# Inverse feature transform in two 64-row lanes: a spectral and attention mixer on one Trainium2 core

## Chip, core and metric

The kernel runs on one core of one Trainium2 chip. The metric is the device time of one execution in microseconds (us). Before the change the median of 3 runs is 452.72 us (452.72 to 453.53).

## What is computed

The input x has 2048 rows (positions) and 640 features. Branch A is attention over 8 dilated neighbours with 32 heads, followed by a 640 x 640 projection. Branch B is a two-dimensional real Fourier transform, a product with complex weights, and the inverse transform. A gate per row mixes the two.

```python
def _B_ref(x, w_r, w_i):
    X = jnp.fft.rfft2(x, axes=(-2, -1))
    X = X * (w_r + 1j * w_i)
    return jnp.fft.irfft2(X, s=(S, D), axes=(-2, -1))

x = A_x
g = _sigmoid((x * gate_w).sum(-1, keepdims=True))
a = _A_ref(x, A_wqkv, A_wo)
b = _B_ref(x, B_w_r, B_w_i)
return g * a + (1 - g) * b
```

## The kernel before

Rows are held as 128 partitions by 16 row groups `j`. The work has four stages, which overlap.

1. `qkv` (lines 445 to 500) multiplies x by the 1920 columns of `wqkv` in three products of rounded halves each; results go to DRAM (`qkvd`). `fold` and `cols` make the first half of the forward transform beside it; its result is `zg`, a tile of 5 blocks of 128 features by 16 row groups by 128 positions.
2. `attend` computes the attention on VectorE (DVE) and GpSimd (POOL); it runs from early on until late, head by head.
3. `freq(g)` for 16 frequency groups `g`: TensorE (PE) transforms features into `u` and `v`, VectorE adds and subtracts them into `ab`, TensorE transforms across row groups into `x` and `z`, both are multiplied by the weights, and the sums and differences of the two halves, `s`, are transformed back across row groups (`g`), and ScalarE (ACT) copies them into `zg` again.
4. `spatial(j)` for 16 row groups: TensorE applies the inverse feature transform. Six matmuls `oa` and `ob` take the five 128-row blocks of `zg[:, t, j]` as stationary operands and the table `gt` as the moving one, ScalarE copies both results to `os`, and four matmuls `ha` and `hb` do the last transform along positions. `project_even` and `project_odd` apply `wo` (`woa`, `wob`), and VectorE and GpSimd add up the output.

In stage 3 `s` is one row of features per frequency: 321 sums P + z and 319 differences P - z, side by side. Five 128-column slices of `s` become the five blocks of `zg`. The sums are cosine terms, first those of the even features and then those of the odd ones, and the differences are sine terms in the same manner, so that a block's 128 rows can hold parts of two kinds. `oa` is made from the cosine terms (blocks 0 to 2) and `ob` from the sine terms (blocks 2 to 4), with all 128 rows each time; block 2 is loaded for both:

```python
mm(o1[:, 0:322], 1, gt[:, 161:483], True, False)
mm(o1[:, 0:161], 0, gt[:, 0:161], False, False)
mm(o1[:, 161:322], 2, gt[:, 483:644], False, True)
mm(o2[:, 0:322], 3, gt[:, 805:1127], True, False)
mm(o2[:, 0:161], 2, gt[:, 644:805], False, False)
mm(o2[:, 161:322], 4, gt[:, 1127:1288], False, True)
```

A float32 matmul is two matmul instructions and two weight loads on TensorE; the profile counts these ("x96" for 16 x 6 matmuls).

What each engine does in which order is not left to a scheduler. Every operation is recorded (`Plan.record`), and `order` puts them into the order that the string `ORDER` holds, a compressed list of positions; all instructions are therefore issued from one line, L385 in the profile, and are told apart by their tiles. Each engine works through its list in that order.

Of the kernel before, what the change touches and what calls it, by code (L numbers as in the profile page):

```python
# [11 lines left out]
AF = mybir.ActivationFunctionType  # L12
# [5 lines left out]
S, D = 2048, 640  # L18
# [13 lines left out]
def dft_tables():  # L32
# [6 lines left out]
    tau = 2 * np.pi  # L39
    ke, ko = PERM[:161], PERM[161:]  # L40
# [87 lines left out]
    def ck(k):  # L128
        return (np.where((k == 0) | (k == 320), 1.0, 2.0) / (S * D))[:, None]

    gt = np.zeros((640, 644))
    gt[0:161, 0:161] = np.cos(tau * np.outer(ke, d) / D) * ck(ke)
    gt[161:321, 161:322] = np.cos(tau * np.outer(ko, d) / D) * ck(ko) * (d < 160)
    gt[321:480, 322:483] = -np.sin(tau * np.outer(kb, d) / D) * ck(kb) * ((d > 0) & (d < 160))
    gt[480:640, 483:644] = -np.sin(tau * np.outer(ko, d) / D) * ck(ko) * (d > 0)
    gt = np.concatenate(
        [gt[0:128, 0:161], gt[128:256, 0:322], gt[256:384, 161:483], gt[384:512, 322:644], gt[512:640, 483:644]], 1
    )
    f = np.float32
    return {  # L140
        "t_fc": np.concatenate([fc, back[0].T, back[1].T], 1).astype(f),
# [94 lines left out]


# [18 lines left out]
class Mixer:  # L256
# [64 lines left out]
    def work(self):  # L321
# [33 lines left out]
        self.bt, self.gt = self.one("bt", 1288, tag="e0"), self.one("gt", 1288, tag="e1")  # L355
        S.dma_start(self.bt[:, 0:1122], ins["t_bt"])
# [280 lines left out]
    def freq(self, g):  # L637
# [77 lines left out]
        d0 = 321  # L715
# [7 lines left out]
        last = s[:, 640:768] if g == 0 else s[:, 512:640]  # L723
        chunks = [[(s[:, 0:128], 0)], [(s[:, 128:256], 0)], [(s[:, 256:384], 0)], [(s[:, 384:512], 1)], [(last, 1)]]
        if g == 0:
            chunks[2:4] = [[(s[:, 384:512], 1), (s[:, 256:321], 0)], [(s[:, 512:640], 1)]]
        for t0, n in ((0, 3), (3, 2)):
            o = self.ps(BG, f"g{g}_{t0}")
            for i in range(n):
                for w, back in chunks[t0 + i]:  # L730
                    m = tb[:, 1024 + 128 * back : 1152 + 128 * back] if g == 0 else tb[:, 192:320]
                    T.matmul(
                        o[0 : w.shape[1], i * 128 : i * 128 + 128],
                        w,
                        m,
                        start=(i == 0),
                        stop=(i == n - 1),
                        skip_group_check=True,
                    )
# [21 lines left out]
    def spatial(self, j):  # L761
# [2 lines left out]
        zg, gt = self.zg, self.gt  # L764
        o1, o2 = (self.ps((0, 1, 2), f"o{i}{j}") for i in "ab")

        def mm(o, t, r, start, stop):
            T.matmul(o, zg[:, t, j], r, start=start, stop=stop, skip_group_check=True)

        mm(o1[:, 0:322], 1, gt[:, 161:483], True, False)  # L770
        mm(o1[:, 0:161], 0, gt[:, 0:161], False, False)
        mm(o1[:, 161:322], 2, gt[:, 483:644], False, True)
        mm(o2[:, 0:322], 3, gt[:, 805:1127], True, False)
        mm(o2[:, 0:161], 2, gt[:, 644:805], False, False)
        mm(o2[:, 161:322], 4, gt[:, 1127:1288], False, True)
# [191 lines left out]
```

## Time and profile before

The profile is of one execution, with a span of 454.1 us from its first instruction to its last; the page gives no other time for that execution. The median of the timed runs is 1.4 us shorter.

| what | value |
|---|---|
| median of 3 runs | 452.72 us |
| span of the profiled execution | 454.1 us |
| moved by DMA, whole span | 110.75 MB, mean 244 GB/s |
| HBM read, written | 72.51 MB, 32.84 MB |
| granted TensorE clock, mean | 0.996 |
| GpSimd busy | 363.9 us (80%) |
| ScalarE busy | 211.9 us (47%) |

In the profile's lists a row names the engine, the operation and the tiles as out<-in, then shapes, the number of instructions, the busy time in us, the mean time of one in ns, and the idle time of the engine ahead of them. PE is TensorE's matmuls, PEld its weight loads, which run beside matmuls. A matmul's own duration is longer than the distance to the next one's start, since they are pipelined; what a queue of matmuls costs is read from the starts.

### The profile page before, as it was taken

To read this page: it belongs to the slowest core of one execution; us is meant where nothing else is said; L and a number is where in the kernel's file an instruction comes from. 1 tells how busy PE (TensorE), PEld (TensorE's weight loads), DVE (VectorE), ACT (ScalarE), POOL (GpSimd) and SP (SyncE) were. 2 spreads that over 40 slices of the span, in tenths; PEclk is the share of its full clock that TensorE was granted. 3 is DMA by queue.
4 is the path that set the end of the run, shared out by engine and by line. 5 is a ranking of instruction groups with operands and counts; after the bars stand their busy time and mean duration, and the time that the engine had idled before them with its cause. 6 is when DMAs were issued, how large, how long until landed. Compare 5 with 4: busy or idle time off the path is not lost. (4 is left out here: it accounts for less than half of the span.)

```text
span 454.1 us, 7249 instructions
## 1 busy us (share of the span) xinstructions
PE 441.2 (97%) x2440; PEld 391.8 (86%) x2440; DVE 409.8 (90%) x519; ACT 211.9 (47%) x561; POOL 363.9 (80%) x316
## 2 busy tenths in 40 slices
PE   9999999999999999999998989999989999999996
PEld 6888888888889888899886769998877899999996
DVE  4899999899999999999978989999999997899484
ACT  4723165625226463255356666667554655342110
POOL 1158895899899898988977898976899998889810
PEclk9999999999999999999998999999999999999999
DMA  8998999887968979679979778989883331365932
GB/s 312 401 383 268 340 330 377 305 264 237 272 183 272 340 217 316 181 216 320 303 220 294 240 230 250 297 245 320 258 257 105 85 97 54 118 207 134 296 123 87
DMA packets 73956, 110.75 MB, mean 244 GB/s; under 512 B 21296, under 2 KB 50992, under 8 KB 73920
## 3 DMA queue, kind: packets, MB, share of 16 engines
q1 hardware_dynamic: 40192, 69.32, 46.8%
q10 hardware_dynamic: 32816, 36.97, 26.1%
q0 software_dynamic: 912, 4.00, 2.4%
q8 instruction: 19, 0.31, 0.3%
q14 instruction: 17, 0.14, 0.1%
HBM read 72.51 MB, written 32.84 MB: 232 GB/s over the span
## 5 line engine op out<-in xcount | busy, mean ns | idle before, releaser
L385 PE MATMUL qkv<-w,xo 128*128 128x480 f32 (+1 forms) x480 | 110.6, 385 | 0.0
L385 PE MATMUL qkv<-w,xe 128*128 128x480 f32 (+1 forms) x474 | 104.3, 382 | 0.0
L385 PEld LDWEIGHTS qkv<-w,xe 128*128 128x128 f32 x474 | 89.3, 189 | 15.2 <-ACT xe L385 0.9
L385 PEld LDWEIGHTS qkv<-w,xo 128*128 128x128 f32 x480 | 89.7, 189 | 13.8 <-ACT zg L385 0.2
L385 ACT COPY ev<-qkv 128x480 f32<-128x480 f32 x64 | 34.9, 558 | 48.3 <-PE qkv L385 35.9
L385 PE MATMUL woa<-wo,oT 128*128 128x320 f32 x240 | 47.2, 318 | 0.4 <-ACT oT L385 0.4
L385 PE MATMUL wob<-wo,oT 128*128 128x320 f32 x240 | 46.9, 315 | 0.2 <-ACT ya L385 0.2
L385 POOL TENSOR_TENSOR P<-P,wp 128x963 f32<-128x963 f32 (+1 forms) x16 | 35.4, 2212 | 6.6 <-DMA P<-X 4.0
L385 PEld LDWEIGHTS woa<-wo,oT 128*128 128x128 f32 x240 | 37.7, 188 | 1.1 <-ACT oT L385 0.6
L385 PEld LDWEIGHTS wob<-wo,oT 128*128 128x128 f32 x240 | 37.8, 188 | 0.6 <-ACT ya L385 0.4
L385 POOL TENSOR_TENSOR fx<-fx 128x160 f32<-128x160 f32 (+1 forms) x16 | 12.8, 818 | 24.2 <-DMA fc<-in_t_fc 17.1
L385 POOL TENSOR_TENSOR w<-raw,w 128x480 fp32r<-128x480 f32 (+1 forms) x20 | 24.8, 1262 | 5.3 <-ACT w L385 5.3
L385 ACT CAST oT<-oTp 128x384 fp32r<-128x384 f32 (+1 forms) x32 | 13.4, 427 | 30.9 <-PE oTp L385 17.3
L385 PEld LDWEIGHTS g<-mm,s 128*128 128x128 f32 x150 | 21.0, 190 | 7.1 <-ACT zg L385 5.0
L385 PE MATMUL g<-mm,s 128*128 128x128 f32 x150 | 23.5, 280 | 3.1 <-ACT zg L385 3.0
L385 DVE TENSOR_TENSOR oT<-oTp,oT 128x384 fp32r<-128x384 f32 (+1 forms) x32 | 15.2, 485 | 11.0 <-ACT oT L385 10.7
L385 PE MATMUL oa<-gt,zg 128*128 128x161 f32 (+1 forms) x96 | 24.0, 344 | 0.0
L385 PE MATMUL ob<-gt,zg 128*128 128x161 f32 (+1 forms) x96 | 22.0, 344 | 0.0
L385 PE MATMUL u<-bt,zc 128*128 128x240 f32 (+2 forms) x96 | 21.1, 335 | 0.7 <-DVE ab L385 0.7
L385 PE MATMUL v<-bt,zc 128*128 128x240 f32 (+2 forms) x96 | 21.5, 335 | 0.2
L385 DVE TENSOR_TENSOR fx<-fx 128x642 f32<-128x642 f32 (+2 forms) x24 | 19.2, 798 | 0.7
L385 PEld LDWEIGHTS u<-bt,zc 128*128 128x128 f32 x96 | 16.9, 199 | 2.9 <-PE g L385 0.9
(304 smaller groups left out, 1107.6 us busy)
## 6 DMA issues: line engine op xcount, KB each, us to landing
qkvd<-ev ACTq DMA_DIRECT2D x32, 480.0 KB, 4.8
wp<-in_ws SPq DMA_DIRECT2D x16, 642.0 KB, 5.9
raw<-in_wqkv SPq DMA_DIRECT2D x25, 240.0 KB, 5.9
fx<-in_x SPq DMA_DIRECT2D x8, 641.0 KB, 7.9
ot<-od SPq DMA_DIRECT2D x16, 320.0 KB, 3.9
P<-X ACTq DMA_DIRECT2D x30, 160.5 KB, 4.6
fd<-fx POOLq DMA_DIRECT2D x6, 640.0 KB, 5.6
f<-fd SPq DMA_DIRECT2D x6, 640.0 KB, 6.1
```

Of the source, the lines that this page charges most:

```text
L385: p.dve.memset(w, 0.0)
```

## The change

The inverse feature transform of stage 4 is laid out anew. Even features and odd features form two lanes of 64 rows: each of the five blocks of `zg` now holds 64 even-feature rows in partitions 0 to 63 and 64 odd-feature rows in partitions 64 to 127. `oa` is made from the lower 64 rows of all five blocks, `ob` from the upper 64 rows. That makes ten matmuls of 64 rows where there were six of 128 rows. Before, the six matmuls of a row group have 1288 output columns in all; now each lane's five have 966, both lanes' ten 1932. `oa` and `ob` still lie in PSUM banks of their own. `gt` is shortened from 1288 to 966 columns, the two copies into `os` keep their number.

To give `zg` that layout, stage 3 writes `s` in four pieces rather than two: 256 sums, 32 + 32 differences, 32 + 32 sums, 256 differences; the zeroth sum is written by one ScalarE activation of a single column. Group 0 clears two 128-column pieces and writes its differences one parity at a time. The number of `g` matmuls stays.

The order string is another one.

```diff
+STRIPS = (2, 0, 322), (0, 0, 161), (1, 0, 161), (3, 161, 161), (4, 161, 161)
...
 ORDER = """
-T>t<81poj4|NsC0{{R31`zHT%QmDPk&^9H>y=H*?`Lk%9Gnl%)B_CdQV7rLsIrdLM6sJFoVB8Rk|2U=URH5DLwHy3}>N|I2375U5sNENOZ_r>p;QjNS0Qt^d&3_BFn1BL!{U(U9<aW#`
...
+{Wp48S^xk5{}S0j0stWa8~^|S5YJf5;2m=f99;ka0sAKZbW*6j%FQ!El~cU`6eXsx^(m8QmuIkq#|cH@ab~Jn4egv)CIlEHgj+~6SGMaZ?}mn0k-S+`iIg>hnOfzJ?024dK1+{_s&$Fa?USIGCMp69
...
+        plus, mixed, minus = (s[:, 128 * t : 128 * t + 128 * n] for t, n in ((0, 2), (2, 1), (3, 2)))
+        plus, minus = (q.rearrange("p (t b r) -> p b t r", t=2, b=2) for q in (plus, minus))
+        mixed = mixed.rearrange("p (b r) -> p b r", b=2)
+        V.tensor_add(plus, strips(P[:, 0], 0), strips(z, 0))
         if g == 0:
-            d0 = 449
-            G.memset(s[:, 384:449], 0.0)
-        V.tensor_add(s[:, 0:321], P[:, 0], z)
-        V.tensor_sub(s[:, d0 : d0 + 319], P[:, 0, 2:], z[:, 2:])
+            other = s[:, 640:768].rearrange("p (b r) -> p b r", b=2)
+            G.memset(s[:, 256:384], 0.0)
+            G.memset(s[:, 640:768], 0.0)
+            for b in range(2):
+                V.tensor_sub(other[:, b, 33 - b : 64], parity(P[:, 0], 1 - b, 31 + b)[:, b], parity(z, 1 - b, 31 + b)[:, b])
+        else:
+            V.tensor_sub(mixed[:, :, 32:64], parity(P[:, 0], 0, 32), parity(z, 0, 32))
+        V.tensor_add(mixed[:, :, 0:32], parity(P[:, 0], 128, 32), parity(z, 128, 32))
+        V.tensor_sub(minus, strips(P[:, 0], 32), strips(z, 32))
+        A.activation(out=s[:, 288:289], in_=z[:, 0:1], func=AF.Identity, bias=P[:, 0, 0:1])
...
-        mm(o1[:, 0:322], 1, gt[:, 161:483], True, False)
...
+        c = 0
+        for t, a, n in STRIPS:
+            for o, k in ((o1, slice(0, 64)), (o2, slice(64, 128))):
+                T.matmul(
+                    o[:, a : a + n], zg[k, t, j], gt[k, c : c + n], start=(t == 2), stop=(t == 4), skip_group_check=True
+                )
+            c += n
         os = self.osr.next(f"os{j}", 644)
-        oq = os.rearrange("p (b a d) -> p a b d", b=2, a=2)
-        A.copy(oq[:, 0], o1[:, 0:322].rearrange("p (b d) -> p b d", b=2))
-        A.copy(oq[:, 1], o2[:, 0:322].rearrange("p (b d) -> p b d", b=2))
+        A.copy(os[:, 0:322], o1[:, 0:322])
+        A.copy(os[:, 322:644], o2[:, 0:322])
```

The order on TensorE at the start of stage 4, before the change. `oa1` is the result `oa` of row group j = 1, `g15` belongs to the last frequency group, the number behind an underscore is the buffer's; the last word is the size of the output:

```order
L385 MATMUL g15_3_815<-mm13_771,s15_813 128x128 x2
L385 MATMUL oa1_872<-gt_327,zg_211 128x322
L385 MATMUL oa1_872<-gt_327,zg_211 128x161 x2
L385 MATMUL oa3_878<-gt_327,zg_211 128x322
L385 MATMUL ob1_873<-gt_327,zg_211 128x322
L385 MATMUL ob1_873<-gt_327,zg_211 128x161 x2
L385 MATMUL oa3_878<-gt_327,zg_211 128x161 x2
L385 MATMUL ha1_875<-os1_874,fct_71 128x161
L385 MATMUL ob3_879<-gt_327,zg_211 128x322
```

The same place on TensorE in the changed kernel, where every `oa` and `ob` row is a matmul of 64 rows:

```order
L385 MATMUL oa3_878<-gt_327,zg_211 128x322
L385 MATMUL oa3_878<-gt_327,zg_211 128x161
L385 MATMUL g15_3_815<-mm13_771,s15_813 128x128
L385 MATMUL oa1_872<-gt_327,zg_211 128x322
L385 MATMUL g15_3_815<-mm13_771,s15_813 128x128
L385 MATMUL oTp0_860<-ident_69,ot12_858 128x128
L385 MATMUL ob1_873<-gt_327,zg_211 128x322
L385 MATMUL oa1_872<-gt_327,zg_211 128x161 x4
L385 MATMUL ob1_873<-gt_327,zg_211 128x161 x3
L385 MATMUL oa3_878<-gt_327,zg_211 128x161
L385 MATMUL ob1_873<-gt_327,zg_211 128x161
L385 MATMUL oa3_878<-gt_327,zg_211 128x161
```

The code emits the lanes in turn, `oa`, `ob`, `oa`, `ob`; the order string does not keep that. Here `oa1` has four of its matmuls in a row, and 128-row matmuls (`g15`, `oTp0`) stand between 64-row ones. Over the whole program the ten matmuls of the 16 row groups make 160; behind 40 of them the next TensorE matmul is one of the other lane, behind 78 one of the same lane, and behind 42 a matmul of 128 rows. TensorE changes 84 times between 64-row and 128-row matmuls.

On VectorE, the place in stage 3 where group 8's `s` is made, before the change (`L5a`, `o6a0` and `pv6a0` are attention, `oT4` is a projection's transpose):

```order
L385 TENSOR_TENSOR z9_729<-z9_729,wp9_718 128x321
L385 TENSOR_REDUCE o6a0_510<-pv6a0_511 128x160
L385 TENSOR_TENSOR z8_716<-z8_716,P8_714 128x321
L385 TENSOR_TENSOR s8_726<-P8_714,z8_716 128x321
L385 TENSOR_TENSOR s8_726<-P8_714,z8_716 128x319
L385 TENSOR_REDUCE L5a_535<-pr5a4_538 128x2x8x4
```

And in the changed kernel:

```order
L385 TENSOR_REDUCE o6a0_510<-pv6a0_511 128x160
L385 TENSOR_TENSOR z8_716<-z8_716,P8_714 128x321
L385 TENSOR_TENSOR s8_726<-P8_714,z8_716 128x2x2x64
L385 TENSOR_TENSOR s8_726<-P8_714,z8_716 128x2x32
L385 TENSOR_TENSOR s8_726<-P8_714,z8_716 128x2x2x64
L385 TENSOR_TENSOR s8_726<-P8_714,z8_716 128x2x32
L385 TENSOR_REDUCE L5a_535<-pr5a4_538 128x2x8x4
```

What stands around the group's `s` is the same; two instructions have become four.

More of the change, by code (lines that the diff above doesn't have):

```diff
@@ L129, in ck @@
         return (np.where((k == 0) | (k == 320), 1.0, 2.0) / (S * D))[:, None]
[L131 to L138, printed above, removed]
+    lanes = np.zeros((2, 320, 322))
+    for lane, k, fits in ((0, PERM[1:161], (d > 0) & (d < 160)), (1, ko, d > 0)):
+        c = np.cos(tau * np.outer(k, d) / D) * ck(k) * ((d < 160) | (lane == 0))
+        s = -np.sin(tau * np.outer(k, d) / D) * ck(k) * fits
+        lanes[lane, 0:160, 0:161], lanes[lane, 160:320, 161:322] = c, s
+    lanes[0, 160] = np.repeat([1.0, 0.0], 161) / (S * D)
+    lanes = lanes.reshape(2, 5, 64, 322)
+    gt = np.concatenate([lanes[:, t, :, a : a + n].reshape(128, n) for t, a, n in STRIPS], 1)
     f = np.float32
@@ new lines @@
+PX7ALwn0<wZc-XUI@uX1mU#xt`{)!LYce^&ssP;n?EzePgxk9JYd-{y%QQy;6@U0P+@zPBuvj7-t=45W#JdGDHIopEeO-jU%d(DaB*?`~N2mvs|1sUot0s7}VMrBB#eDFDo1RKH`%ZVCAxAl3(^&}7
+=ii?a-c4VPi7pf#6?m=5bcslwsyM3(R8$%(MJtAn_Uay(Im|tR^~RuuetfDSu^OE{tfa6ps`>u^-kX`B#A~Vwsc%SjY;Jv92jN3lgge|M0vo2qX)bXSpjst7E>PIJ<7MEo%zVLW&X?8{G4=k07HU|a
+*MB}kJYv|NIbH5jPR0w-0Fa4K>I-_70~`#r(KRi^7WJrck|i_3^8gN95G9AXi4lNxH=tv50Oxq7r{pPjmK#$_p#v6^rnt-ge<m+NSkr_@vcHb6MXsjb?W55?t9?PjGDmpF#nG~xLUBY<#IB>k!h$C!
+z-hlt+~emyEO0bO{wwJEu1hR3X1@N0OrQxh{JF$lk}G3NGs%?Yg#!@iY8_EH7!(?|4h|x;tC|ye+sgvGErvgz0esf}QvSK!V<W(<VfxlLS&4~}O`Bk0{oQyhED2T(^C#jqPq!2(`dv=hHRXC?DG029
@@ new lines @@
+SLk6^a_aagp?qPWw@h5GUtaNZ&W&Bj8fsg6^0)ykAEdVUHu~dkqQz~s?J*y0XyY7m&e2o<4i_=Q0#iEbAi7WG1FM|jik?-qV)4y!?9rePIO#p`BXZX*@r*QUL%z6H+$jP!{aVZm_rW+PbfI{9bG*U?
+E_LINx}Qna>NY+WBy4?@jhjD=la(qlzBu?W$|nb!jA$dZ-?H4`6$Q&w`N~!ZeO+mgilZS?4hij#%}oqVUXoE<Pblzkdc<6|_77YecmZD2Tg-0!H6snUTdLYCZVrNVu<X^Sh}J$|!9HGI_gki@@!oYb
+c4wLL50)gM?0juDa}iV3@FJm+NVn9Vs$3m61ycd31-y?kN{<RAdAOHWx$*HvG^p93wpc%naJrrMa>fV(DF7o}7%YSpO(sbtu4-fo6hNAOTd);|!L$CzhR+=Hf*jY`F!e30j#$*$;Q)Z&C-h~7m=O<R
+fjSLesvd}MFN%#rz%9yh%V6CFi2)X|8&!a^uXS^-5+Dz;BgC--$QFdndlcJ}x=myp!sjM~9tN1)Gb77g>UT5D05%2%-@g+RnEpaadJ#4Py3Qv}L5%N_SXpUuTJH!`0SM@u*h9t$eE-|R%mNLEm;(qs
@@ new lines @@
+uyj39*(7WO{+@C){tWJiHK+1eH4IEvha9nJm}{<iH2>4_UT2#!Li8j@1xqDi#Wp&s@C+VfdqMMlg>cIPOdof~zzvANxeA1%O;s{)#g~{NP_$Yna;Q`LYzlE5orJ=$uC}dhb*ffVv`Ng6e~bDe!(vya
+A9{8KX7mR#!a}~8<#?fxEye_3fTTM43mhddtO8&6isL=MD34oI_-)P*AfC4AVzS0Q?mUeVONAl&F-ijQMPx}tAU<*%mcz<M)Kud>S^ik151vBL%=7%StnMzBYjr@@ihnvR_~Ke{5{hi;J1*PRa9f8P
+cf{tPut3EXfiAw#VBY9x0MAWLa{oADt{4ZSey4!=iu$b`<HXdv0I?SgFg||D2dR9v=v(H9E3aMVyFxtX9zJ#M#q8}?N+{P%l8QWVW|3A1k67584Nvh#kdCjVc5O!+;-!nPPdDE6T(3-Y@bSM+VgHt^
+xZw_S6@%Rf$pL>I%p9Q;>B;_FjwPrab<uIXx_ZB7Fuyv=khT6^+d#6T@|G>_WIkC<Q)h`AxwMC^+`pBX@@pwRL-Ts5tpXt3b9B4Z3<ruB(HupyzD)MIcBcw74!XpjjGlW{VAdSd4To|Ac%rJ)Z67|u
@@ new lines @@
+`b_Bs5RS{WkWL4-t<u_OO0L(I-&zr~G-3Q0&CF&u(1F`YWedb=>~XE1Eh=KEd+k=_)R2B0;P_aen3$+Y%#*M%Z-b~Dq<;HUY%&2}HJFKNc@)MP!t6s^y$tMG733C~T<!y#!<E5mgNuPAS7~?cK@}B_
+$xTpaxh^#|add$WS1z5dt|f}*DNka~bbvi&V<y~i9nuioNR4K4zM+!)0G1fpD;%n#s3*irf6tDad7qU!D%VZTD^?!G0T}~CYCt%mU4zq^6MM&LHRBHu-`zgW51yn>=!97yh)7BjhKc+yuFt<KUL=^j
+s90G+PUsk~tp^iqelS4lhT!>mC<^{2Bz?@SAvF-AIwCzfF0_k+;DyYam@35NBWWhchi`r|u9@M-L9)wUC);%}fj%U6&smz{4&Z158Pr#OY(){xh(YeOijOD|?o7vpG5Qk%q7aP*3X67E+9U?dTo3_%
+OhBtc#S&NE-odH$dXI2h=GbsO57Ns1onb0!_*ld|2(0nCbzuSbbYi#>&txzrqZa7Eup?8MkprbK8WX1A?pC$^3aDYk^B44^2sv32i_S7+e6Nn}Sw*?LK&SY%jCoP(^zrc(gz@tg6tMA=E~sK4H}ebm
@@ new lines @@
+Yx6`jtOV1lwULSH-rcwzn^%t76@dUQov5+W`X{0iz}qQO8I3W&1d!r!>5rEr!q4AxRh1^qdA`5Ki~H5O$6^(fH3O6UM4@jO^XdO?3YAOKvN+-D0enc7!AWr?I7Gr4i4?I=$oC$Q@=z@&j(~F8J<IG3
+2aRj3Hfur$9dJhL8JzionfUczGlv8WpsKs}MOCmIGid2&*R9|en!i_XXR8U@n-n$G;SD5tVT~CNbSVL(KL^Ls2{Y^pJD%H|8zHHh9wSl&y6>Lm&>>>6Xnwr#e=NP&Q?&#r$24f@e17F%$N10+W`|la
+O%_$H@Qtzk%=kB;&%XwRV`kJSAH|1x_Ku5N**gJ&OB!Q0#b*-9kv-uS5nd;>8f$}SG<&AMx=1tj)nZCC$BlN8^6JDFJqxxktod*I4A5Vp`H8Z((Nt43>%eaPY#0Qwg43eS<om(Ds~_c~#>$o}6YFgP
++w8vX%L^GJoYqvY)TUMxy*i>7EQ>y<Ge7Ns6h|@yY6r(~-B8=}q?NG$kv!t%mEK2}zC|o5Oiwe8POu|nMo9m3U#G}J$iG3ZuL2b_gTOcd<MPRKQ(V#IE%2x{?)!kppDvm$ZOS3J9}UeKZXPHVZ#ki`
@@ new lines @@
+-Ma{L0BwyV*v_V9Vp6JYA+xp;O?+&@agHN}#!tYU0r`LmIa|L8l;j5l7Pc%k@Y>zbmk#dK1y?peo9?rel;N{45vkL{+J30!Xq!ipgaR^+wFaJps#zBqzlxyso~+8E?{-cZsDIEnG)SSUtZp=u8%fO0
+x#z-KrE`@E;TO^L8&UUC(x}AwM<f`qT|0^F)#C&1HW5kwIkY23kpt=c&0b>f*RhW+47rj@;F==oSaG+y9IZYZ7B|d@Je&A_+;j+<MeR#(TEO8WIUxD8lXhbF#fHKqKDfe;xQozxH+V#}7l;?1Lrq9t
+;-xb|+AFP$Oa;-ou2&8LBffSVvzV*M_FR1byB-z9@%u%t)-aBY^}>mqqsJOT+1+MZv&A&8q?$A}w%_{>Pa8Kz?d$fbG?X9+vm{rzjz-^#q8pak^KtdHr{z5=(pljljw}`cTeX4|tq<9mE%?!8SkiSF
+z<c{e441L_pl`j+h~yJ;lla;tU=e<$G{S;Gq9Zh|GYENB(}hK9EVc2-F4S)^Si?E?Bj>-PydaGMk}(d<S3r&*8p|6L^5;p*Xc)e!*zIPA<_kYy<$)MA{;6mt_WyZmgF~S&gvo=n`=Na#>o`-=W>09!
@@ L235 @@
+KPXOqH<$%PPC*HYQL2_1V1h=yrM2>Sia5KKBhf+XJYyN@o%-VfsYSLDJ!>)Ed--@im0`D%ELn1NE37TJZA37uJXQe`gH{PUZ}J(FyeQEiL@c1stf(5QN7HSeO;@iczt+qkJ%in(?jNCu?)RUbRyoqv
+`D16Tk8)c4|Ij8O5SOZp855l%7Huf?Z9`qNRWkur9U_2?J+<W*Y&_r{GA)TZyi`(#%H_Z<;`nQ=|Hd@&{ct2lE-8SS^%Z~xswN|PGhQ)Vg^knG4z}PX^z~lfT(@;bO$q0+>8sg-st{g_zKvWr=W-@u
+7ibO4^CC=zgKx~}_2ys$yiEjVG)97Z%+w_S00FQX^f~|lJ*hX-r~nH50ssI2003E9
 """
@@ L354, in work @@
         S.dma_start(self.sign, ins["t_sign"])
-        self.bt, self.gt = self.one("bt", 1288, tag="e0"), self.one("gt", 1288, tag="e1")
-        S.dma_start(self.bt[:, 0:1122], ins["t_bt"])
+        self.bt, self.gt = self.one("bt", 1122, tag="e0"), self.one("gt", 966, tag="e1")
+        S.dma_start(self.bt, ins["t_bt"])
         S.dma_start(self.gt, ins["t_gt"])
@@ L714, in freq, with parity, strips @@
         s = self.s12r.next(f"s{g}", 768)
-        d0 = 321
-        if g == 0:
-            d0 = 449
-            G.memset(s[:, 384:449], 0.0)
-        V.tensor_add(s[:, 0:321], P[:, 0], z)
-        V.tensor_sub(s[:, d0 : d0 + 319], P[:, 0, 2:], z[:, 2:])
+        def parity(a, k, n):
+            return a[:, 1:321].rearrange("p (b k) -> p b k", b=2)[:, :, k : k + n]
+        def strips(a, k):
+            return parity(a, k, 128).rearrange("p b (t r) -> p b t r", t=2)
+        plus, mixed, minus = (s[:, 128 * t : 128 * t + 128 * n] for t, n in ((0, 2), (2, 1), (3, 2)))
+        plus, minus = (q.rearrange("p (t b r) -> p b t r", t=2, b=2) for q in (plus, minus))
+        mixed = mixed.rearrange("p (b r) -> p b r", b=2)
+        V.tensor_add(plus, strips(P[:, 0], 0), strips(z, 0))
+        if g == 0:
+            other = s[:, 640:768].rearrange("p (b r) -> p b r", b=2)
[8 more added lines that the diff above has]
+        A.activation(out=s[:, 288:289], in_=z[:, 0:1], func=AF.Identity, bias=P[:, 0, 0:1])
         yield
[L723 to L726, printed above, removed]
         for t0, n in ((0, 3), (3, 2)):
@@ L729, in freq @@
             for i in range(n):
-                for w, back in chunks[t0 + i]:
+                for t, back in (((0, 0),), ((1, 0),), ((2, 0), (5, 1)), ((3, 1),), ((4, 1),))[t0 + i][: 2 if g == 0 else 1]:
                     m = tb[:, 1024 + 128 * back : 1152 + 128 * back] if g == 0 else tb[:, 192:320]
                     T.matmul(
-                        o[0 : w.shape[1], i * 128 : i * 128 + 128],
-                        w,
+                        o[:, i * 128 : i * 128 + 128],
+                        s[:, 128 * t : 128 * t + 128],
                         m,
```

39 lines of the change are left out of this document (2 added, 37 removed).

## Prediction

> **What bounds the kernel now.** I read the head of the page first, then the chain of work that ended last, then the busy time of each engine by stage.
>
> ```profile
> span 454.1 us, 7249 instructions
> PE 441.2 (97%) x2440; PEld 391.8 (86%) x2440; DVE 409.8 (90%) x519; ACT 211.9 (47%) x561; POOL 363.9 (80%) x316
> ...
> by line: PE woa L385 6.9%; PE wob L385 6.4%; PE oa L385 3.8%; PE ob L385 3.8%; PE hb L385 1.9%; PE ha L385 1.9%; PE g L385 1.8%; PE oTp L385 1.2%; DMA P<-X 0.7%; PE v L385 0.7%; DVE o6a L385 0.6%; ACTq L385 0.6%; DVE pr5b L385 0.6%; PE x L3
> ...
> core 0: us, PE busy (x) PEld busy (x) DVE busy (x) ACT busy (x) POOL busy (x), PEclk, DMA share, GB/s
> 0.00:220.00 220.00, 218.94 (x1068) 189.91 (x1069) 206.22 (x207) 99.07 (x250) 177.91 (x163) 1.00 0.87 291
> 220.00:347.40 127.40, 119.83 (x706) 105.57 (x705) 117.51 (x173) 76.22 (x217) 109.32 (x85) 0.99 0.84 259
> 347.40:409.00 61.60, 61.60 (x386) 56.26 (x385) 55.28 (x75) 29.88 (x78) 54.71 (x45) 1.00 0.34 103
> 409.00:454.10 45.10, 40.84 (x286) 40.02 (x284) 30.78 (x68) 6.68 (x16) 22.00 (x25) 1.00 0.51 161
> ```
>
> TensorE (PE) is busy for 441.2 of 454.1 us, and the chain's shares are nearly all PE rows. The last four rows split the span where the change splits it: the qkv stage (to 220), the frequency groups (220 to 347.4), the inverse feature transform with its last step (347.4 to 409), and the last projections. From 347.4 to 409 PE is busy 61.60 of 61.60 us: **each us that its `oa` and `ob` matmuls gain or lose there is a us of the kernel**, until another engine takes over. The next is VectorE (DVE) with 55.28 us. From 220 to 347.4 neither is full: PE has 7.6 us idle, DVE 9.9 us.
>
> **The matmuls of the inverse transform.** What one costs is the distance between starts:
>
> ```profile
> start us, us, engine line op out<-in xcount [idle before <-releaser]
> 378.07 0.44 PE L385 MATMUL hb<-os,fct 128*128 128x161 f32 x2
> 378.34 0.43 PE L385 MATMUL oa<-gt,zg 128*128 128x161 f32 x2
> 378.61 0.44 PE L385 MATMUL ha<-os,fct 128*128 128x161 f32 x2
> 378.89 0.70 PE L385 MATMUL oa<-gt,zg 128*128 128x322 f32 x2
> 379.43 0.71 PE L385 MATMUL hb<-os,fct 128*128 128x161 f32 x4
> ```
>
> A pair of instructions (one float32 matmul) of 161 columns takes 378.34 to 378.61, 0.27 us; one of 322 columns takes 378.89 to 379.43, 0.54 us. Before, `oa` has one wide and two narrow matmuls in each of 16 row groups, and `ob` the same: 32 x (0.54 + 2 x 0.27) = 34.6 us, and the chain's 3.8% + 3.8% of 454.1 us is 34.5 us. The change removes these and adds, for each lane and row group, one wide and four narrow ones of 64 rows: 32 x (0.54 + 4 x 0.27) = 51.8 us if they run one behind the other, 25.9 us if the two lanes always run side by side. So this part lies **between +17.2 and -8.7 us**. No row of the trace shows a matmul of 64 rows, so both ends stand; the order decides where between them it falls.
>
> Between, I take a walk through the changed order with two rules: a matmul instruction starts no earlier than the one ahead of it on PE, and no earlier than its own lane is free; one of 128 rows needs both. The first rule is what the rows above show, where each instruction starts as the last one's 0.135 us are over, in the program's order. Then four `oa1` in a row hide nothing: `ob1` behind them starts when the last instruction of the fourth starts. Only at a change of lane does an instruction of the one run beside the last of the other. There are 40 such changes; each hides one instruction, 0.135 us where both are narrow and up to 0.27 where both are wide; walked through, 6.2 us in all. 51.8 - 6.2 = 45.6 us, or **+11.0 us** against 34.6. Lanes in strict turn would have hidden almost half of 51.8; the order, with 78 same-lane successors against 40, does not let them. I take the walk, since it uses the spacing of the nearest rows and their order.
>
> A rule speaks about the two assumptions. The Trainium skill ("TensorE: Matmul & The Clock Gate", section "The mechanism") says that matmuls of different row groups overlap, starting some 4 ns apart, and that matmuls start and end in program order. No run here shows the first; by both together the sum is the walk's.
>
> Weight loads grow from 12 to 20 instructions per row group, and could become a bound themselves:
>
> ```profile
> L385 PEld LDWEIGHTS oa<-gt,zg x96: 187/190/192, 347.4 to 406.9; 128*128 128x128 f32 x96
> L385 PE MATMUL oa<-gt,zg 128*128 128x161 f32 x64 | 13.5, 299 | 0.0
> L385 ACT COPY z<-qkv 128x1 f32<-128x1 f32 x16 | 2.5, 162 | 1.7 <-ACT ev L385 1.7
> ```
>
> A load takes 190 ns and there is one every 135 ns already, with no idle PE time in the `oa` row (0.0), so loads are pipelined as well. Beside the run of one lane they are hidden as now; where two lanes do pair, two loads are needed in 135 ns, which no row shows. At worst the pairing then hides nothing: that is the +17.2 end.
>
> **The group sums.** Distances between starts on DVE:
>
> ```profile
> 337.04 0.42 DVE L385 TENSOR_TENSOR oT<-oTp,oT 128x256 fp32r<-128x256 f32 x1 [0.38 <-ACT oT L385]
> 337.38 0.49 DVE L385 TENSOR_TENSOR z<-z,wp 128x321 f32<-128x321 f32 x1
> ...
> 339.97 0.87 DVE L385 TENSOR_TENSOR s<-P,z 128x321 f32<-128x321 f32 x2
> 340.76 0.41 DVE L385 TENSOR_REDUCE s5a<-L5a 128x32 f32<-128x256 f32 x1
> ...
> 342.48 0.34 DVE L385 RECIPROCAL s5a<-s5a 128x32 f32<-128x32 f32 x1
> 342.74 1.43 DVE L385 TENSOR_TENSOR pr4a<-kt4a,qbank 128x1280 f32<-128x1280 f32 x1
> ```
>
> Two instructions of 321 and 319 columns take 339.97 to 340.76, 0.79 us. In their place come two of 256 (0.34 each, 337.04 to 337.38) and two of 64. For 64 I extrapolate: 0.395 for 320 and 0.34 for 256 columns make 0.055 per 64 columns, so 0.34 - 3 x 0.055 = 0.18; the shortest small one in these rows, 32 columns, takes 0.26, which I take as the upper end. A group costs 2 x 0.34 + 2 x 0.18 = 1.04 us, +0.25 (up to +0.41); 16 groups +4.0 us (0 to 6.6). DVE has 9.9 us idle in that stage and waits for other engines in some of it, while PE waits for DVE in other places; the front shows that nothing else moved around `s`. I put **+1.4 us** of the 4.0 on the path, a third, with 0 and 6.6 as ends. What stands behind `s` on DVE is attention (`L5a`), which GpSimd and the odd projections wait for; that work has room in the longer stage that follows.
>
> The 16 one-column activations on ScalarE are 16 x 0.162 = 2.6 us by the row of the one-column copy `z<-qkv`. ScalarE is busy 76.22 of 127.40 us there; behind each stand copies into `zg` and `zc`, so 0 to 2.6, and I take 0 (inside the 1.4). The copies into `os` keep number and size; the 128-column memsets on GpSimd run once, and GpSimd has 18 us idle in that stage: 0. `gt` is a quarter shorter and loaded long ahead: 0. The qkv stage has the same instructions in another order, PE busy 218.94 of 220: 0, ends -1 and +1.
>
> **Sum.** +11.0 + 1.4 = +12.4 us in the profiled execution, 454.1 to 466.5; the median of the runs stands 1.4 us below the span, so **465.1 us**.
>
> **Rivals.**
> 1. *The lanes do not overlap at all* (two loads in 135 ns do not fit, or float32 pairs block each other; then the change doesn't do what its name says). Against it only that nothing in the trace forbids it. +17.2 + 1.4: **471.3**.
> 2. *Switching between 64-row and 128-row matmuls empties the array.* TensorE changes 84 times. An `oa` instruction lasts 299 ns in the row above and the next starts after 135; if the next had to wait for the end, that is 0.164 us each, 84 x 0.164 = 13.8 us on top of the walk: **478.9**. The trace has no such switch. The Trainium skill ("TensorEngine Tiling (Array Packing)", section "Key Properties") says that a change of tiling mode drains TensorE; by that rule this rival is the forecast, without it the walk is, and no run here shows it yet.
> 3. *Lanes with queues of their own*, each running ahead of the other between two matmuls of 128 rows. Walked through so, 13.3 us are hidden rather than 6.2, and `oa` and `ob` cost 38.5 us, +3.9: **458.0**. Against it: PE's rows start in program order.
> 4. *Faster: each 64-row matmul costs half, whatever the order*, because PE takes matmuls of the idle lane from far behind in its queue, past 128-row ones. -8.7 on PE; but DVE, with 55.28 of 61.60 us, then ends the stage: at most -6.3, and +1.4: **447.8**. It decides from the point at which more than 17.2 + 1.4 = 18.6 of the 25.9 us that can be hidden are hidden. For it: weight loads run ahead of matmuls already (PEld busy 56.26 us beside a full PE), so PE looks ahead in some way; against it: rival 3's reason, and the 84 barriers.
>
> **How the numbers follow.** The walk gets 0.42, no overlap 0.17, draining 0.14, own queues 0.10, half cost 0.14, and 0.03 is left for a new order that gains or loses elsewhere (PE has 12.9 us idle in the span, which a better order could use). The forecast is the likeliest case, 465.1. The range 455 to 480 holds the first four (0.83) with the bounds of the sums below and above them, but for the case that draining and the upper bounds meet; it leaves out the faster case. A measurement of this kernel can tell about 0.2% from no change (0.9 us; the three runs lie 0.8 apart). Slower: 0.82; within 0.2%: 0.03 (something between rivals 3 and 4); faster: 0.15.
>
> **What would show it.** If the walk is right, `oa` and `ob` starts in the new trace lie 0.135 us apart within a run of one lane, two starts come nearly together only at a change of lane, and the stage from the first `oa` to the last `ha` grows by about 11 us with PE full. No pairs of near starts at all: rival 1. A gap of some 0.16 us whenever a `woa`, `ha` or `g` follows an `oa` or `ob`: rival 2. Starts of 64-row instructions 0.07 us apart on average: rival 4, and the forecast is wrong on its main term. `s` rows: four per group with about 1.04 us from first start to the next instruction. If PE idles more than 2 us longer between 220 us and the first `oa`, the 1.4 was too small.

## Result and profile after

The changed kernel takes 479.92 us (median of 4 runs, 479.33 to 481.69) against 453.12 us: the ratio is 1.0593, 95% interval 1.057 to 1.0616. It is 26.8 us slower. The forecast was 465.1 us, 12.4 us slower; the direction was right, the size less than half.

The head of the changed kernel's page:

```profile
span 477.6 us, 7544 instructions
PE 464.9 (97%) x2568; PEld 398.0 (83%) x2568; DVE 411.7 (86%) x552; ACT 215.3 (45%) x577; POOL 362.1 (76%) x317
```

Its busy time by stage; the columns are those of the windows shown before, with the borders moved to the first `oa` and the last `ha`:

```profile
core 0: us, PE busy (x) PEld busy (x) DVE busy (x) ACT busy (x) POOL busy (x), PEclk, DMA share, GB/s
0.00:220.00 220.00, 216.37 (x1051) 186.58 (x1052) 203.58 (x203) 95.34 (x237) 172.63 (x161) 1.00 0.88 286
220.00:348.60 128.60, 123.29 (x720) 105.80 (x718) 123.59 (x209) 82.41 (x244) 114.35 (x90) 1.00 0.87 263
348.60:434.60 86.00, 86.00 (x527) 66.84 (x527) 54.52 (x76) 31.84 (x82) 53.50 (x43) 1.00 0.25 78
434.60:477.60 43.00, 39.26 (x274) 38.80 (x273) 30.05 (x66) 5.68 (x15) 21.64 (x25) 1.00 0.55 169
```

The loss is in one row. The inverse transform took 62.5 us before (first `oa` at 347.5, end of the last `ha` at 410.0) and takes 86.0 us now, with TensorE full in both; the stages ahead of it are 1.1 us longer, the one behind it 1.1 us shorter. That makes 23.5 us of span. The timed runs differ by 26.8. The changed kernel's profiled run took 479.33 us for a span of 477.6, 1.7 us more; by the same step (an estimate) the span of before belongs to a run of 455.8 us, 2.7 above the median. The granted TensorE clock of before, the third number from the end, has a dip ahead of the inverse transform that the changed kernel's profile does not have:

```profile
240.00:260.00 20.00, 17.81 (x86) 14.99 (x87) 18.17 (x29) 12.65 (x38) 15.33 (x15) 0.91 0.89 276
```

If those 2.7 us were lost ahead of the transform, the stages there have really grown by 3.8 us rather than 1.1; the profiles do not settle it. Of the runs below, two of the four of e4_same took 528.9 and 529.8 us at a mean granted clock of 0.93 and 0.92, of which there is no profile, and its time, stage and ratio are those of the other two.

What happened to the matmuls shows in the timeline of TensorE. Rows are start, length, engine, operation and tiles; `ha` and `hb` have 128 rows, `oa` and `ob` 64:

```profile
361.18 0.82 PE L385 MATMUL hb<-os,fct 128*128 128x161 f32 x4
361.93 0.54 PE L385 MATMUL ob<-gt,zg 64*128 64x322 f32 x1
361.94 0.54 PE L385 MATMUL oa<-gt,zg 64*128 64x161 f32 x2
362.31 0.43 PE L385 MATMUL ob<-gt,zg 64*128 64x322 f32 x1
362.31 0.43 PE L385 MATMUL oa<-gt,zg 64*128 64x161 f32 x2
362.58 0.98 PE L385 MATMUL ob<-gt,zg 64*128 64x161 f32 x6
...
366.18 0.54 PE L385 MATMUL ha<-os,fct 128*128 128x161 f32 x2
366.65 0.54 PE L385 MATMUL oa<-gt,zg 64*128 64x161 f32 x2
367.12 0.82 PE L385 MATMUL hb<-os,fct 128*128 128x161 f32 x4
```

Two things stand here. At 361.93 and 361.94 both lanes start 7 ns apart: they do run side by side, and `ob`'s second instruction (362.31) starts after `oa`'s second, though it stands ahead of it in the program. And around a change between 128 and 64 rows things are slow: `ha` at 366.18 and `oa` at 366.65 are single narrow matmuls, which took 0.27 us from start to start before; each takes 0.47 us here. The weight loads of the same place, with their idle time in brackets:

```profile
366.18 0.30 PEld L385 LDWEIGHTS ha<-os,fct 128*128 128x128 f32 x2 [0.17 <-issue]
366.65 0.29 PEld L385 LDWEIGHTS oa<-gt,zg 64*128 64x128 f32 x2 [0.17 <-issue]
367.12 0.57 PEld L385 LDWEIGHTS hb<-os,fct 128*128 128x128 f32 x4 [0.17 <-issue]
```

The load of each first matmul behind a change starts with that matmul and not ahead of it, after 0.17 us without any load. The load no longer hides behind the matmul before. In the rows of the tile `oa` (shortest, median and longest in ns; x96 are 16 x 3 float32 matmuls of two instructions) this is the maximum. The kernel before:

```profile
L385 PE MATMUL oa<-gt,zg x96: 297/300/437, 347.5 to 407.0; 128*128 128x161 f32 x64, 128*128 128x322 f32 x32
```

The changed kernel:

```profile
L385 PE MATMUL oa<-gt,zg x160: 294/298/536, 348.6 to 431.9; 64*128 64x161 f32 x128, 64*128 64x322 f32 x32
```

A wide instruction lasts 535 or 536 ns behind a change, where the longest of before lasted 437: 0.10 us of a weight load waited for. The other 0.09 us lie ahead of it, in which nothing starts: `ha` at 366.18 and `oa` at 366.65 are 0.47 us apart: 0.27, 0.10 for the load and 0.09, rounded. Together a change costs about 0.19 us, and there are 84.

### The profile page after: what moved, and what is told of

Same layout as the page of the kernel before. It is cut to its first block, busy times and chain, and to the rows that moved or that the text cites. A ratio compares the mean times of both kernels' runs of the same rounds, so it can differ in the third digit from the quotient of the medians.

```text
span 477.6 us, 7544 instructions
## 1 busy us (share of the span) xinstructions
PE 464.9 (97%) x2568; PEld 398.0 (83%) x2568; DVE 411.7 (86%) x552; ACT 215.3 (45%) x577; POOL 362.1 (76%) x317
## 4 chain that ended last, share of the span: by engine, by line
PE 76%; DVE 5%; POOL 4%; DMA 2%; ACT 2%; issue 2%; ACTq 0%; POOLq 0%; SPq 0%; DVEq 0%
PE qkv L385 33%; PE woa L385 7%; PE wob L385 7%; PE oa L385 5%; PE ob L385 5%; PE z L385 5%; DVE fx L385 3%; PE g L385 3%; PE hb L385 2%; POOL P L385 2%; PE ha L385 2%; PE u L385 2%; PE oTp L385 2%; PE v L385 2%; DMA wp<-in_ws 2%
## 5 line engine op out<-in xcount | busy, mean ns | idle before, releaser
L385 PE MATMUL qkv<-w,xo 128*128 128x480 f32 (+1 forms) x480 | 116.0, 389 | 0.0
L385 PE MATMUL qkv<-w,xe 128*128 128x480 f32 (+1 forms) x474 | 106.3, 383 | 2.6 <-ACT ev L385 1.8
L385 PEld LDWEIGHTS qkv<-w,xo 128*128 128x128 f32 x480 | 88.5, 189 | 12.8 <-ACT zg L385 0.2
L385 PE MATMUL wob<-wo,oT 128*128 128x320 f32 x240 | 49.6, 324 | 0.6 <-ACT ya L385 0.6
L385 PE MATMUL oa<-gt,zg 64*128 64x161 f32 (+1 forms) x160 | 34.7, 344 | 0.6 <-ACT zg L385 0.6
L385 PE MATMUL ob<-gt,zg 64*128 64x161 f32 (+1 forms) x160 | 34.5, 345 | 0.0
L385 POOL TENSOR_TENSOR fx<-fx 128x160 f32<-128x160 f32 (+1 forms) x16 | 11.7, 741 | 22.4 <-DVE fx L385 19.4
L385 PEld LDWEIGHTS oa<-gt,zg 64*128 64x128 f32 x160 | 23.5, 186 | 5.7 <-issue 3.1
L385 ACT CAST oT<-oTp 128x384 fp32r<-128x384 f32 (+1 forms) x32 | 13.3, 428 | 32.9 <-PE oTp L385 32.0
L385 PEld LDWEIGHTS ob<-gt,zg 64*128 64x128 f32 x160 | 23.6, 186 | 4.6 <-issue 3.2
L385 PE MATMUL g<-mm,s 128*128 128x128 f32 x150 | 25.4, 282 | 0.8 <-ACT zg L385 0.8
```

What stands on the lines that cost most here:

```text
L385: p.dve.memset(w, 0.0)
```

## Experiments

All times of a run are medians (of e4_same both); ratios are to runs of the kernel before on the same chip beside them, which took 453.1 to 454.2 us. The stage is from the first `oa` to the end of the last `ha` or `hb` in the run's profile, as above.

| run | time, us | ratio, 95% interval | stage, us | changes 64/128 rows |
|---|---|---|---|---|
| before | 453.12 | 1 | 62.5 | none |
| changed | 479.92 | 1.0593 (1.057 to 1.0616) | 86.0 | 84 |
| e1_turns | 465.99 | 1.0249 (1.0179 to 1.032) | 70.8 | 30 |
| e2_runs | 492.75 | 1.0839 (1.0771 to 1.0907) | 98.0 | 30 |
| e3_full | 475.82 | 1.0471 (1.041 to 1.0532) | 81.1 | none |
| e4_same | 490.1, 491.0 | 1.0792 (1.0696 to 1.0888) | 97.2 | 84 |
| e5_pipe | 461.85 | 1.0166 (1.0124 to 1.0208) | 67.9 | 30 |
| e6_split4 | 455.67 | 1.0034 (1.0007 to 1.0062) | 62.5 | none |
| e7_old_order | 466.71 | 1.0261 (1.0216 to 1.0306) | 69.0 | 30 |
| e8_copies | 463.28 | 1.0192 (1.0157 to 1.0226) | 67.0 | 30 |
| e9_old_copies | 460.24 | 1.0151 (1.0122 to 1.0181) | 63.9 | 30 |

### e1_turns: the lanes in turn, nothing between

TensorE's order, the first row group (the other engines' order stays):

```diff
-L385 MATMUL ob1_873<-gt_327,zg_211 128x322
-L385 MATMUL oa1_872<-gt_327,zg_211 128x161 x4
-L385 MATMUL ob1_873<-gt_327,zg_211 128x161 x3
+L385 MATMUL oa1_872<-gt_327,zg_211 128x322
+L385 MATMUL ob1_873<-gt_327,zg_211 128x322
+L385 MATMUL oa1_872<-gt_327,zg_211 128x161
+L385 MATMUL ob1_873<-gt_327,zg_211 128x161
...
```

> The changed kernel with one thing different: the ten 64-row matmuls of each row group stand together on TensorE, the two lanes in turn, with no 128-row matmul among them (30 changes between 64-row and 128-row matmuls in place of 84; nothing else is moved). Theory A (lanes run from queues of their own between 128-row matmuls, and every change costs about 0.195 us: 0.09 us in which the array empties and 0.105 us of an exposed weight load): oa and ob cost 26.0 + 30 x 0.195 = 31.9 us against 38.7 + 84 x 0.195 = 55.1 in the changed kernel, so 479.9 - 23.2 = about 457. Theory B (program order holds between lanes, a change of lane hides one instruction, changes cost what then remains, 0.11 us): 28.2 + 3.3 = 31.5, about the same; the next run tells them apart. Theory C (the loss lies elsewhere, in the new order of the other engines): at most 5 us faster than the changed kernel.

465.99 us: 13.9 us faster than the changed kernel, but 9 us short of theory A; theory C is out. The timeline of its first row group:

```profile
350.53 0.27 PE L389 MATMUL oTp<-ident,ot 128*128 128x128 f32 x1
350.74 0.54 PE L389 MATMUL oa<-gt,zg 64*128 64x322 f32 x1
350.74 0.54 PE L389 MATMUL ob<-gt,zg 64*128 64x322 f32 x1
351.11 0.43 PE L389 MATMUL oa<-gt,zg 64*128 64x322 f32 x1
351.12 0.43 PE L389 MATMUL ob<-gt,zg 64*128 64x322 f32 x1
351.38 0.30 PE L389 MATMUL oa<-gt,zg 64*128 64x161 f32 x1
351.39 0.30 PE L389 MATMUL ob<-gt,zg 64*128 64x161 f32 x1
...
352.35 0.29 PE L389 MATMUL ob<-gt,zg 64*128 64x161 f32 x1
353.16 0.54 PE L389 MATMUL ha<-os,fct 128*128 128x161 f32 x2 [0.51 <-ACT os L389]
```

In turn, the lanes lose nothing: 20 instructions start in pairs, and the group, from its first start until the last pair at 352.35 has had its 0.135 us, takes 1.75 us, 1.63 us of it the sum of one lane (one wide and four narrow matmuls) and 0.10 us the first weight load. The first step, 350.74 to 351.11, is 0.37 us where a wide instruction takes 0.27. What theory A had not counted is the last row: `ha` waits for ScalarE's copy into `os`, 0.51 us, since nothing stands between any more. TensorE is idle for 6.4 us in this stage, where before it has no such wait: 2.6 us end with a copy into `os`, 2.8 us with ScalarE's scalings `ho` and `h` of the last results, 1.0 us with other work. Starts of `ha` and `hb` lie 219 and 201 ns from the next start on average, changes included; before it is 136.

### e2_runs: one lane first, then the other

```diff
-for t, a, n in STRIPS:
-    for o, k in ((o1, slice(0, 64)), (o2, slice(64, 128))):
+for o, k in ((o1, slice(0, 64)), (o2, slice(64, 128))):
+    for t, a, n in STRIPS:
```

(The order string does it; these lines say what it amounts to.)

> As the run before (30 changes, matmuls of a row group together), but the five of one lane first and then the five of the other. Theory A (queues of their own): the second lane's matmuls start beside the first lane's, as fast as in turns: about 457. Theory B (program order holds, only one instruction in each group is hidden): oa and ob cost 16 x (3.26 - 0.14) + 30 x 0.11 = 53 us, about 478.

492.75 us. Queues of unlimited depth are out. The first row group:

```profile
351.55 1.50 PE L391 MATMUL oa<-gt,zg 64*128 64x322 f32 x7
352.75 0.54 PE L391 MATMUL ob<-gt,zg 64*128 64x322 f32 x1
352.88 0.43 PE L391 MATMUL oa<-gt,zg 64*128 64x161 f32 x2
353.13 0.43 PE L391 MATMUL ob<-gt,zg 64*128 64x322 f32 x1
353.16 0.29 PE L391 MATMUL oa<-gt,zg 64*128 64x161 f32 x1
353.40 1.26 PE L391 MATMUL ob<-gt,zg 64*128 64x161 f32 x8
```

Seven of ten `oa` instructions start alone; `ob` comes in when three are left. All 14 groups of this run that stand alone start in this pattern: **here TensorE looks ahead past three waiting matmul instructions of the busy lane, no more**. (Whether their weight loads count too, no run tells.) A group takes 2.95 us in place of 1.75. Per group the run lies between the theories (1.75 and 3.12 us), near theory B; its time is 15 us beyond theory B's 478, since the waits of e1_turns and a lower clock come on top.

At full clock the order of the lanes explains 18 us of the 26.8 between this run and e1_turns. Most of the rest is the clock: three groups of the stretch below take 4.7, 5.6 and 5.6 us rather than 2.95, 7 us in all.

```profile
370.00:380.00 10.00, 8.77 (x47) 7.42 (x46) 7.59 (x7) 1.99 (x7) 7.37 (x6) 0.83 0.00 0
380.00:390.00 10.00, 10.00 (x34) 8.02 (x34) 0.00 (x0) 3.15 (x8) 1.84 (x2) 0.50 0.20 49
390.00:400.00 10.00, 10.00 (x37) 9.05 (x37) 8.79 (x7) 0.71 (x4) 4.65 (x4) 0.50 0.07 18
```

The third number from the end is the granted clock of TensorE: 0.50 for 20 us, with TensorE shown busy throughout. In the changed kernel's profile it is 1.00 in every stage.

### e3_full and e4_same: overlap and changes apart

```diff
 # e3_full
-o[:, a : a + n], zg[k, t, j], gt[k, c : c + n], start=(t == 2), stop=(t == 4), skip_group_check=True
+o[:, a : a + n], zg[:, t, j], gt[:, c : c + n], start=(t == 2), stop=(t == 4), skip_group_check=True
 # e4_same
-for o, k in ((o1, slice(0, 64)), (o2, slice(64, 128))):
+for o, k in ((o1, slice(0, 64)), (o2, slice(0, 64))):
```

> The changed kernel and order, but the ten matmuls of a row group take all 128 rows of zg and gt, so that both lanes' products are added up in both results (the inverse transform's values are left out in that sense); the number, width and place of the matmuls stay. No lane can run beside another and there is no change between 64 and 128 rows. Theory A: oa and ob cost 32 x 1.628 = 52.1 us against 55.1, 3 us faster than the changed kernel: about 477. If changes cost nothing (my prediction's walk), 52.1 against 45.6: 6 us slower, about 486. If a change costs 0.16 us on top of the walk: 52.1 against 59.4, 7 us faster, about 472.5.

> The changed kernel and order, but both results are made from the lower 64 rows of zg and gt, so that the odd features are left out and the even ones are computed twice; number, width and place of the matmuls stay, and the 84 changes stay, but there is one lane only and nothing can run side by side. Theory A: 52.1 + 84 x 0.195 = 68.5 us against 55.1, 13.4 us slower than the changed kernel: about 493. The distance to the run with all 128 rows is the price of 84 changes: 16.4 us by theory A, 0 if changes are free, 9 by theory B.

e3_full takes 475.82 us, 4.1 less than the changed kernel; e4_same takes about 490.5. Both are near theory A. The rows of the tiles `oa` and `ha` of e3_full:

```profile
L385 PE MATMUL oa<-gt,zg x160: 297/300/538, 350.0 to 428.7; 128*128 128x161 f32 x128, 128*128 128x322 f32 x32
L385 PE MATMUL ha<-os,fct x64: 297/300/303, 355.4 to 430.9; 128*128 128x161 f32 x64
```

And of e4_same:

```profile
L385 PE MATMUL oa<-gt,zg x160: 294/297/536, 349.1 to 443.6; 64*128 64x161 f32 x128, 64*128 64x322 f32 x32
L385 PE MATMUL ha<-os,fct x64: 297/300/404, 355.2 to 445.9; 128*128 128x161 f32 x64
```

`ha` is the same matmul in both. Its maximum is 303 ns among 128-row matmuls and 404 ns behind 64-row ones: the change costs in both directions. (The 538 ns of e3_full are the first `oa`, which had waited 0.57 us for `zg`, so that its load too started with it.) With the same instructions in the same places, the stages are 81.1 us without changes and 97.2 us with 84 of them: 16.1 us, **0.19 us per change**; 0.09 and 0.10 us, read from the starts and lengths, make the same. The changed kernel has 86.0 with the 84 changes and two lanes: the overlap hides 97.2 - 86.0 = **11.2 us**. And with all 128 rows, one behind the other, the stage is 81.1 - 62.5 = **18.6 us** longer than with the six matmuls of before. 17.0 us of this are the matmuls themselves: from start to next start `oa` and `ob` take 34.5 us before and 51.5 in e3_full. The rest is other work, since the new order has nine more matmul instructions `oTp` and `g` inside this stage (about 1.0 us). 18.6 + 16.1 - 11.2 = 23.5 us, the whole difference of the stage.

### e6_split4: the four sums alone

```diff
-        V.tensor_add(s[:, 0:321], P[:, 0], z)
-        V.tensor_sub(s[:, d0 : d0 + 319], P[:, 0, 2:], z[:, 2:])
+        V.tensor_add(s[:, 0:257], P[:, 0, 0:257], z[:, 0:257])
+        V.tensor_add(s[:, 257:321], P[:, 0, 257:], z[:, 257:])
+        V.tensor_sub(s[:, d0 : d0 + 64], P[:, 0, 2:66], z[:, 2:66])
+        V.tensor_sub(s[:, d0 + 64 : d0 + 319], P[:, 0, 66:], z[:, 66:])
```

> The kernel before, with the two VectorE instructions that make a group's sums and differences cut in two each, at the same place in the order (257 + 64 and 64 + 255 columns; the same values). This is the cost of the four parts by itself, without lanes, layout or another order. My prediction's term: 1.04 rather than 0.79 us per group on VectorE, 4.0 us in all, a third of it on the path: 1.4 us, about 454.5. Bounds 453.1 and 457.

Ratio 1.0034 (1.0007 to 1.0062): 1.5 us, between 0.3 and 2.8, of ten runs from 453.9 to 459.8. Its profile does not show where: the first `oa` starts at 347.2, and not later than before (347.5). In the changed kernel's timeline of VectorE the four instructions and what follows them:

```profile
321.15 1.02 DVE L385 TENSOR_TENSOR s<-P,z 128x64 f32<-128x64 f32 x4
322.08 0.55 DVE L385 TENSOR_TENSOR oT<-oTp,oT 128x384 fp32r<-128x384 f32 x1
```

0.93 us against 0.79, so 0.14 us more per group and not the 0.25 of the prediction: 2.2 us in 16 groups rather than 4.0.

### e5, e7, e8, e9: can the lanes be made to pay

e5_pipe starts from e1_turns, e7_old_order from the order of before; in both the next row group's ten matmuls go ahead of this one's `ha` and `hb`. e8_copies and e9_old_copies also put ScalarE's copies right behind their group. The order of the blocks, G for the ten matmuls, c for the copies, H for `ha` and `hb`:

```diff
-G1 H1 G3 H3 G5 H5
+G1 G3 H1 G5 H3 G7 H5
 # e8, e9 also
+G1 c1 G3 c3 H1 G5 c5 H3
```

> As the run with the lanes in turn, with one more thing moved: the ten matmuls of the next row group stand ahead of the ha and hb matmuls of this one, so that TensorE has work while ScalarE copies oa and ob (in the run before, ha and hb took 23.9 us between starts in the stage rather than 15.6, which is 8.3 us of waiting for these copies). 30 changes between 64 and 128 rows as there. Theory A (two lanes at full speed when they stand in turn, 0.19 us per change): oa and ob cost 26.0 + 30 x 0.19 = 31.7 us and the 8.3 us of waiting go: 466.0 - 8.3 = about 457.5. Rival (the waiting only moves: the third PSUM bank of oa and ob is not free when the next group stands there): 463 or more.

> The changed kernel's work in the order of the kernel before: each group's four sums stand where its two stood, each row group's ten lane matmuls stand together and in turn ahead of its first copy, and the next group's ahead of ha and hb. 30 changes. Theory A: oa and ob 31.7 us against 34.5 before, 2.8 us less, and the four sums cost up to 1.4: about 452, a little faster than the kernel before. Rival (the searched order is worth something on the other engines): as slow as or slower than the pipelined run with the new order.

> As the pipelined run, with ScalarE's two copies of a row group right behind its ten matmuls in the order, ahead of the scalings of the row group before. Theory A (what is left over the bound of 26.0 + 30 x 0.19 us is TensorE waiting for these copies, 4.0 us in gaps of over half a us): 461.9 - 4 = about 458. Rival (the waits come from somewhere else, the banks of ha and hb for instance): 461 or more.

> The same on the order of the kernel before. Theory A: its gaps of over half a us are 7.6 us in the profile, 466.7 - 7 = about 459.5 or less; with the old order's earlier first oa (347 against 349 us) it can come down to the kernel before plus the 1.5 us of the four sums, 455. Rival: 465 or more.

461.85, 466.71, 463.28 and 460.24 us. e5 won half of what theory A gave it, whose 8.3 us of waiting for copies had also held changes and the waits for scalings. e7 was expected at 452 and is nearly 15 us above, as its rival had it: as in e1, TensorE waited for copies that the old order had left far behind (3.9 us), and e9, which moves the copies too, gets some 6 us back and comes near its theory A. e8 won nothing on e5, so there the rival holds. e9 has the shortest stage of all lane runs, 63.9 us:

```profile
348.60:412.50 63.90, 61.97 (x519) 52.54 (x519) 55.39 (x76) 29.51 (x79) 53.74 (x44) 1.00 0.33 100
```

Even here it is longer than the 62.5 us of before. What TensorE waited for in this stage, in us, times and the longest:

```profile
PE hb L391 <- ACT ho L391: 1.0, 2, 0.5
PE hb L391 <- ACT h L391: 0.5, 2, 0.3
PE wob L391 <- ACT ya L391: 0.4, 1, 0.4
```

Most of these waits are for ScalarE's scalings `ho` and `h`, which free the one PSUM bank of `hb`. They do not make up all that stands above 62.5 - 2.9 = 59.6 us (the 2.9 are worked out below); the rest is not assigned. None of these versions beats the kernel before. With 30 changes the lanes' own cost is 26.0 + 30 x 0.19 = 31.7 us against 34.6, so by this estimate a gain of 2.9 us is the most that this arrangement can give, and about 1.5 us of that goes to the sums.

## Why the prediction was right and wrong

**The bound** was right: TensorE is full in the stage in both profiles, and the 23.5 us that the stage grew are the whole growth of the span. VectorE, the next, has 54.5 us in a stage of 86.

**Ten matmuls one behind the other, +17.2,** were right: 17.0 from start to start (e3_full). The stage grew by 18.6, because other work moved into it.

**The walk, -6.2, failed in its rule.** It let a lane start only in program order, as the rule does that the prediction sets beside it, so that a change of lane hides one instruction. Between the lanes that order does not hold: three waiting instructions of the busy lane can be passed (e2_runs), and the changed order hides 11.2 us. The same walk with three passed instructions allowed hides 11.9 us, an estimate worked out on the order of starts in e4_same, whose single lane keeps the program's order. Rival 3, with queues of any depth and 13.3 us, erred the other way. Lanes in turn hide one of the two lanes whole (e1_turns), as the prediction had it.

**The price of a change, put at 0, is the step that made the forecast wrong.** The prediction had it as rival 2, with 0.164 us from the length of an instruction less the distance of starts, and a chance of 0.14, because no row showed a change. It is 0.19 us, 84 times: 16.1 us. The sentence of the Trainium skill ("TensorEngine Tiling (Array Packing)", section "Key Properties") that a change of tiling mode drains TensorE agrees with the trace in so far as nothing starts for about 0.09 us. That the array is empty by then the trace does not show: `oa` at 366.65 starts 0.07 us ahead of the shown end of `ha`, and shown ends are modelled. The other 0.10 us, a weight load that does not run ahead of the change, was in none of the rivals.

Rival 2's 478.9 us lies 1 us from the measurement, but by errors that cancel. It hid 5.0 us too little, charged 2.3 us too little for changes, left out the other work in the stage (1.4 us net) and had 1.4 us for the sums, and so came out 2.7 us above the measured span.

**The step from the span to the time of the runs, -1.4,** was wrong as well, for every case alike: it is +2.3 in the changed kernel (477.6 to 479.92), and in each experiment the profiled run took 1.7 to 2.0 us longer than its span. The sum started from a span that, by the estimate above, is 2.7 us too long for the median of before. These 3.7 us bring rival 2 back to 478.9. That the time still lies inside the range, at its upper end, is luck too: the walk did not put it there.

**Two loads in 135 ns** were a worry for pairs; e1_turns shows both lanes at 0.135 us per instruction with a load each, so that rival 1 is out.

**The group sums, +1.4,** are not refuted: 1.5 us by themselves (e6_split4, 0.3 to 2.8), the first `oa` 1.1 us later in the changed kernel. The near agreement is partly luck, since a group costs 0.14 us and not 0.25. The one-column activations last 0.26 us, not 0.162; no run has them alone.

**The faster rival** needed 18.6 us hidden; 11.2 were, and 16.1 had to be paid for.

Still open: how much a better arrangement could win. Two row groups in one block throughout would halve the changes, but need a fourth PSUM bank for `oa` and `ob`, which `ha` holds; it was not tried. One such double block stands in each run with 30 changes, with three banks: in e1_turns and e9_old_copies it takes 4.26 us until the next full matmul starts, where two single blocks take 2 x 1.84 us; the second group's `ob` starts late there. Why e2_runs' clock stays at 0.50 is not settled either.

## What to carry to other kernels

In these runs row lanes double TensorE's speed only for matmuls that stand in turn, lane by lane: behind a run of one lane the other waits until three instructions are left. Every change between lane matmuls and full ones costs about 0.19 us, one and a half narrow instructions of this kernel, so the matmuls between two changes must save more than both cost: here ten save 0.54 us against before, and two changes take 0.38 of it. An order made without these two prices can undo the gain; measure the price of a change first, with a run that has the changes and no overlap, and one that has neither.

## What the runs showed of the hardware that was not expected

- Starts are not in program order across lanes: in e2_runs `ob` passes three waiting `oa` instructions, in the changed kernel `oa`'s second instruction starts ahead of `ob`'s second, which stands before it.
- A change between 64 and 128 rows costs in both directions: `ha` lasts up to 404 ns behind lane matmuls, 303 elsewhere; a wide `oa` up to 536 ns, 437 before.
- In e2_runs the granted clock stayed at 0.50 from 380 to 400 us while TensorE was shown busy for all of it, mostly with one lane of 64 rows at a time.
